# Attention and MLP on one core: weights of 64-key blocks laid as [hi | lo], two products in place of three, and a new plan

## The chip, the cores and the metric

The kernel runs on one core of a Trainium2 chip. The metric is the time on the device of one execution in microseconds, the median of three runs. Five engines run side by side: TensorE (PE; its weight loads are shown apart, as PEld), VectorE (DVE), ScalarE (ACT), GpSimd (POOL), and SyncE (SP), which issues all transfers here.

## What is computed

Eight batches, eight heads, 576 positions of 64 features: attention with a mask by blocks of 64 (a query sees its own block of keys and those before it), then for all 4608 tokens a layer of 512 to 2048 with h * tanh(softplus(h)), and one back to 512. All in float32.

```python
scores = scale * np.matmul(q, k.transpose(0, 1, 3, 2))
mask = block_i >= block_j                  # block = position // 64
scores = np.where(mask, scores, -1000000000.0)
attn = np.exp(scores - np.max(scores, axis=-1, keepdims=True))
attn = attn / (np.sum(attn, axis=-1, keepdims=True) + 1e-09)
x = np.matmul(attn, v)                     # heads side by side: 4608 x 512
h = x @ w_in
g = h * np.tanh(np.log1p(np.exp(h)))
out = g @ w_out
```

## The kernel before

Products of two float32 matrices are made of float16 parts: each operand is split into hi and lo, and hi*hi, hi*lo and lo*hi are summed on TensorE. Batch 0 is an exception; its attention runs in float32 while the weights are loaded and split. For batches 1 to 7, heads are taken in pairs, four pairs a batch, 28 pairs in all. For a pair:

- `load_pair` loads q, k (`ql`, `kl`) and v (`VL`, L850) and splits them: hi by ScalarE or VectorE (L909, L913: `QH`, `KH`, `VH`), lo by VectorE (L917: `QL`, `KL`, `VO`). `VL` has 7 blocks of 128 rows of v: 0 to 2 are full, 3 holds two separate blocks of 64 keys, and 4, 5, 6 hold one block of 64 keys with zeros in the other half. `VH` has a column of ones for the sums of the weights, zero where the keys are.
- `attend_pair` runs the 576 queries in three rounds r = 0, 1, 2. Scores go to PSUM (L1202, L1214), VectorE takes the maxima (L1243, L1251), ScalarE the exponentials into a float32 tile `pe` (L1277). The weights are split into hi and lo by one operation each of 1024 columns for two heads: hi on ScalarE, VectorE or GpSimd (L1309, L1314), lo on VectorE (L1326). Both stand in a tile `P` (`P2`), and a DMA transposes it into `PT` (L1333), keys on the partitions. The last 64 queries of round 1 are transposed once more, as "r = 3", into `PL` (L1348).
- `values` (L1381) multiplies the transposed weights with v: `SEEN` lists, for each half, the blocks (round, block of weights, block of v) that each group of 128 queries sees. Each of them takes three products per head: hi with `VH`, hi with `VO`, lo with `VH`. A block of weights has 128 columns of keys; where only 64 of the keys belong to it, v has zeros in the other half (blocks 4, 5, 6).
- `weigh` divides by the sums and splits the result into `xt`, which a DMA transposes into `x`.

The MLP of 576 tokens is two tiles of 384 and 192 tokens: `m1` (L1559), the activation on ScalarE (L1588), the split into `Gt` (L1620, L1629, L1635), `m2` (L1664), and the store.

No order is written out by hand. Every step is an `Op` with an engine (some with a choice of engines), an estimated duration, and what it comes after. `Plan` gives each a due time out of the table `DUE`, runs a list schedule by these, and emits all engines' queues in the order that comes out. So the numbers in `DUE` alone set which step stands before which in each queue. Tiles are handed around in rings: two `pe`, two `P2`, four `PT`, one `PL`, two score tiles `ss`, one `u`.

Of the kernel before, what the change touches and what calls it, by code (L numbers as in the profile page):

```python
# [30 lines left out]
    "w": ((-61.5, -2, 296, 15.5), (96.5, 301, 329, 293.5)),  # L31
    "batch": (134.5, 54, 455.5, 305.5, 387.5, 808, 492, 726.5),
    "load": (
        (83.5, -32, 600.5, 570),
        (36, 483.5, 361.5, -83.5),
        (276, 346.5, 611, 481.5),
        (565, 598, 494.5, 672.5),
        (648.5, 658, 422.5, 604),
        (343, 499, 528.5, 422.5),
        (661.5, 543, 581, 672),  # L40
        (519.5, 843, 510.5, 637.5),
        (757.5, 795, 760, 591.5),
    ),
    "tile": (
        (-51, -125.5, -73.5, -80.5, -51, -47.5, -51, -26.5,
         319, 223.5, 300.5, 333, 81.5, -56.5, 375,
         314.5, 398.5, 467, 26.5, 342, 505.5, 522),
        (19.5, 249.5, 135.5, 297.5, 196.5, -21.5, 316, 400.5,
         604.5, 539.5, 679, 458.5, 343, 123.5, 283.5,
         267, 250.5, 470, 358, -216, 356.5, -75),  # L50
        (320, 282.5, 449, 284, 681, 964, 780, 427,
         447, 435.5, 624, 399.5, 375.5, 484, 386.5,
         320.5, 409.5, 543, 531.5, 375, 412.5, 340),
        (483, 31, 275.5, 339.5, 292.5, 104, 293, 625,
         84.5, 303.5, 373.5, 407, 379.5, -72.5, 127,
         404, 404.5, 421, 565.5, -125.5, 356, -251.5),
        (448.5, 373.5, 590, 365.5, 434.5, 336.5, 446.5, 284,
         357.5, 489.5, 428, 310, 292.5, -42, 410,
         513.5, 777.5, 590, 613, 604, 709.5, 639.5),
        (372.5, 551, 292.5, 381.5, 476.5, 835, 556, 396.5,  # L60
         724, 871, 821, 711.5, 554.5, 463.5, 309,
         893, 680.5, 615, 529, 515, 441.5, 30),
        (373, 388, 435, 502.5, 260, 301.5, 656.5, 579,
         297.5, 503, 548, 528, 666, 511, 332,
         627, 392, 426, 519.5, 752, 584.5, 605.5),
        (368, 598.5, 373, 367.5, 583, 554.5, 411, 406,
         237.5, 328.5, 607.5, 573, 674.5, -33.5, 787,
         729, 772.5, 818.5, 923.5, 63.5, 469.5, -66),
        (389, 453, 304.5, 478, 715, 634, 371.5, 693.5,
         348, 796.5, 774, 602.5, 855.5, 503, 530,  # L70
         776, 701.5, 819, 590, 813, 895, 812.5),
        (634.5, 956, 494.5, 795, 1165, 830.5, 1058, 709,
         710, 839.5, 692.5, 741.5, 725, 247.5, 944.5,
         560, 629.5, 1001, 527.5, -160, 671, -106),
        (802.5, 973, 1047, 434.5, 658.5, 854, 632, 826,
         762, 798, 686, 941, 746.5, 271.5, 1046.5,
         667, 865, 1006, 611, 643, 1168.5, 645),
        (832, 643.5, 951.5, 1059, 547.5, 819, 763.5, 866,
         699, 730.5, 1083.5, 1171.5, 1010.5, -12, 856,
         594.5, 1149, 860.5, 1071.5, -34, 790, -55.5),  # L80
        (944.5, 712, 595.5, 736, 871.5, 785.5, 960.5, 607,
         692, 788, 586.5, 1165.5, 977.5, 12.5, 753,
         572.5, 900.5, 937.5, 839.5, 768.5, 725.5, 796.5),
        (1028.5, 640, 726, 558, 695.5, 664, 1160.5, 1140.5,
         1094.5, 925, 768.5, 853, 1007, -98, 1008,
         1061.5, 723, 870, 774.5, -89, 1203.5, 261.5),
        (950.5, 896.5, 636, 989.5, 884, 689.5, 926, 1069,
         955.5, 1107, 1099.5, 940.5, 677.5, -156, 1045.5,
         851.5, 705.5, 754.5, 1035.5, 839, 1052, 1161),
        (794, 1058.5, 678.5, 694.5, 811.5, 1135, 639, 810.5,  # L90
         937.5, 1100.5, 1138.5, 870.5, 1130.5, -151.5, 1101,
         876, 1045, 1214.5, 1347.5, 355.5, 1319.5, 461),
# [255 lines left out]
def attention_moe(  # L348
# [87 lines left out]
    PL = [const.tile([P, 4, P], F16, name=f"PL{i}") for i in range(NPL)]  # L436
# [382 lines left out]
    def load_pair(b, p, i, wait_s, wait_u):  # L819
# [80 lines left out]
        v_part = VL.rearrange("p c (a d) -> p c a d", d=D), m["VH"][:, :, :, 0:D], m["VO"]  # L900
        for j, (parts, s, ns, after) in enumerate((
            (q_parts, sc[:, 0:1], (S - 64, P), [sco]),
            ([(kl, m["KH"], m["KL"])], sc[:, 1:2], (S,), [sco]),
            ([v_part], s_x, (KV * P,), [batches[b]["sx"]] + v_ins + wait_u),
# [10 lines left out]
            def lows(parts=parts, s=s):  # L915
                for src, hi_, lo_ in parts:
                    nc.vector.scalar_tensor_tensor(  # L917
                        out=lo_, in0=src, scalar=s, in1=hi_, op0=ALU.mult, op1=ALU.subtract
                    )
# [8 lines left out]
            lo = add("dve", sum(dve(n) + 0.06 for n in ns), lows, [hi])  # L928
# [31 lines left out]
    def attend(p, half, st):  # L960
# [133 lines left out]
        for a in range(2):  # L1094
# [81 lines left out]

    SEEN = (
        (
# [3 lines left out]
        ),  # L1182
        (((0, 0, 0), (0, 1, 5)), ((1, 0, 5),)),
    )

    def attend_pair(b, p, st):
# [83 lines left out]
        for r in range(3):  # L1270
# [33 lines left out]
            def both(r=r):  # L1304
                t = P2[his[r].slot].rearrange("p (k z a q) -> p z a k q", z=2, a=2, q=P)
                return t[:, 0], t[:, 1], pe[ex[r].slot].rearrange("p (a k q) -> p a k q", a=2, q=P)

            def part(op, both=both):
                return lambda: op(out=both()[0], in_=both()[2])  # L1309

            hi = add(
                "act",
                act(1024) + 0.09,
                lambda both=both: nc.scalar.copy(both()[0], both()[2]),  # L1314
# [3 lines left out]
                    ("dve", dve(1024, fast=True), part(nc.vector.tensor_copy)),  # L1318
                    ("pool", 1.05, part(nc.gpsimd.tensor_copy)),
# [5 lines left out]
                dve(1024) + 0.08,  # L1325
                lambda both=both: nc.vector.tensor_sub(both()[1], both()[2], both()[0]),  # L1326
# [17 lines left out]
            if r == 1:  # L1344
                late = add(
                    "sp",
                    TURN_LATE,
                    lambda: nc.sync.dma_start(  # L1348
                        out=PL[late.slot][:, :, 64:P],
                        in_=P2[his[1].slot][64:P, 0 : 4 * P],  # L1350
                        transpose=True,
                    ),
                    [lo, tr],
                    take=[pl_ring],
                    free=[(p2_ring, hi)],
                )
                tr.free, tr.frees = [], []
                last["T"] = late
# [3 lines left out]
        for half in (1, 0):  # L1362
# [3 lines left out]
            def values(half=half, seen=seen):  # L1366
# [3 lines left out]
                for j, bs in enumerate(seen):  # L1370
                    for a in range(2):
                        for r, k, vb in bs:
                            if r == 3:
                                h, l = (PL[late.slot][:, 2 * z + a] for z in range(2))
# [3 lines left out]
                            o = uv[:, j, a]  # L1378
                            vh, vo = m["VH"][:, vb, a], m["VO"][:, vb, a]
                            for out, p_, v_ in ((o, h, vh), (o[:, 0:D], h, vo), (o, l, vh)):  # L1380
# [12 lines left out]
                products([E] * (6 * sum(len(x) for x in seen))),  # L1393
# [339 lines left out]
    TURN, TURN_LATE, TURN_X = (2.7, 0.5), (1.3, 0.3), ((3.8, 0.9), (1.4, 0.5))  # L1733
# [100 lines left out]
```

## Time and profile before

| | us |
|---|---|
| median of three runs | 1007.91 (1007.24 to 1011.48) |
| the profiled execution | 1007.62 |
| its span, first to last instruction | 1005.5 |
| TensorE busy | 986.4 |
| ScalarE busy | 664.4 |
| VectorE busy | 662.2 |
| GpSimd busy | 83.5 |

The span is what the trace shows; 2.1 us lie around it. Busy times are of the whole span, over stages with different limits: until about 140 us the weights are prepared and batch 0 runs, then pairs and MLP tiles run mixed, and after about 850 us only MLP is left. Matmuls overlap, so the duration of one is not what one costs.

### The profile page before, as it was taken

The numbers are of one execution on the slowest core, as the hardware profiler recorded it, in microseconds if no ns is written. First come the engines' busy times: TensorE is split into PE (matmuls) and PEld (weight loads), VectorE is DVE, ScalarE is ACT, GpSimd is POOL, SyncE is SP. The second block draws the span as 40 slices with busy tenths as digits, with TensorE's granted clock in tenths as the row PEclk, the third lists the DMA queues.
The fourth block names the chain that finished last, engine by engine and source line by source line (L and its number), as shares of the span: only waits on it lengthen the run. The fifth ranks groups of instructions, "written<-read, shape, count | busy, mean of one in ns | idle before, by whom it ended". The sixth has DMA issues, their size and how long they took to land.

```text
span 1005.5 us, 25329 instructions
## 1 busy us (share of the span) xinstructions
PE 986.4 (98%) x10856; PEld 734.6 (73%) x10856; DVE 662.2 (66%) x1288; ACT 664.4 (66%) x1042; POOL 83.5 (8%) x111
## 2 busy tenths in 40 slices
PE   8999899999999999999999999999999999999998
PEld 6677467786678688686778766877678866877787
DVE  5999998989878527875469677885568784220210
ACT  2769887768869747777579676885858676332221
POOL 1000311102000001100001010110011210000000
PEclk9999899999999999999999999999999999999999
DMA  9763657796568326693486936693358843320000
GB/s 324 245 191 109 167 101 164 150 198 120 119 147 157 77 36 162 137 195 62 86 147 135 181 77 137 139 179 52 72 120 165 142 93 65 61 56 1 25 17 25
DMA packets 276850, 121.59 MB, mean 121 GB/s; under 512 B 224513, under 2 KB 262913, under 8 KB 276737
## 3 DMA queue, kind: packets, MB, share of 16 engines
q1 hardware_dynamic: 276736, 119.96, 54.5%
q8 instruction: 85, 1.39, 0.6%
q14 instruction: 29, 0.23, 0.1%
HBM read 55.18 MB, written 9.44 MB: 64 GB/s over the span
## 4 chain that ended last, share of the span: by engine, by line
PE 87%; DVE 8%; ACT 2%; issue 2%; DMA 1%; SPq 1%; DVEq 0%; ACTq 0%
PE acc L1664 36%; PE acc L1559 33%; PE u L1381 7%; PE ss L1202 5%; PE u L1139 2%; DVE Gt L603 1%; PE ss L1067 1%; DVE pv L1243 1%; DVE P L1326 1%; PE acc L996 1%; DMA PT<-P 1%; PE acc L667 1%; DVE wo_l L694 1%; PE ss L996 1%; PE ss L1106 0%
## 5 line engine op out<-in xcount | busy, mean ns | idle before, releaser
L1559 PE MATMUL acc<-x,wi_h 128*128 128x192 f16 (+1 forms) x2048 | 393.5, 287 | 0.7 <-DVE ot L1696 0.3
L1664 PE MATMUL acc<-Gt,wo_h 128*128 128x192 f16 (+1 forms) x2048 | 383.7, 286 | 2.2 <-DVE ot L1696 1.2
L1559 PE MATMUL acc<-x,wi_l 128*128 128x192 f16 (+1 forms) x1024 | 293.8, 287 | 0.0
L1664 PE MATMUL acc<-Gt,wo_l 128*128 128x192 f16 (+1 forms) x1024 | 292.9, 286 | 0.0
L1559 PEld LDWEIGHTS <-wi_h 128*128 128x128 f16 x2048 | 191.1, 98 | 81.3 <-issue 5.8
L1664 PEld LDWEIGHTS <-wo_h 128*128 128x128 f16 x2048 | 187.5, 98 | 54.3 <-issue 4.3
L1588 ACT ACTIVATE Et<-acc,bv 128x384 f32<-128x384 f32 x192 | 109.0, 578 | 106.1 <-PE acc L1559 105.2
L1277 ACT ACTIVATE pe<-ss,pv 128x192 f32<-128x192 f32 (+1 forms) x280 | 148.7, 605 | 18.5 <-DVE pv L1251 10.5
L1635 DVE SCALAR_TENSOR_TENSOR Gt<-Et,bv,Gt 128x1536 f16<-128x1536 f32 (+1 forms) x64 | 90.8, 1425 | 105.4 <-ACT Gt L1620 105.2
L1664 PEld LDWEIGHTS <-wo_l 128*128 128x128 f16 x1024 | 100.2, 98 | 34.3 <-issue 1.3
L1559 PEld LDWEIGHTS <-wi_l 128*128 128x128 f16 x1024 | 100.5, 98 | 33.6 <-issue 0.8
L1243 DVE TENSOR_REDUCE pv<-ss 128x2 f32<-128x384 f32 (+4 forms) x140 | 106.0, 790 | 19.1 <-PE ss L1214 18.7
L1326 DVE TENSOR_TENSOR P<-pe,P 128x1024 f16<-128x1024 f32 x84 | 102.9, 1225 | 12.7 <-ACT P L1314 7.6
L1381 PEld LDWEIGHTS <-PT 128*128 128x128 f16 x2352 | 79.7, 98 | 4.7 <-issue 0.6
L1381 PE MATMUL u<-VH,PT 128*128 128x65 f16 x1568 | 82.8, 194 | 0.0
L1381 PE MATMUL u<-VO,PT 128*128 128x64 f16 x784 | 79.4, 193 | 0.0
L1277 ACT ACT_TABLE_LOAD x57 | 73.1, 1283 | 8.4 <-DVE pv L1251 5.5
L1588 ACT ACT_TABLE_LOAD x59 | 75.7, 1283 | 1.0
L1620 ACT ACTIVATE Gt<-Et,bv 128x768 f16<-128x768 f32 (+1 forms) x53 | 64.8, 1224 | 15.7 <-PE acc L1664 14.6
L1703 ACT ACTIVATE ot<-acc,bv 128x384 f32<-128x384 f32 (+1 forms) x37 | 17.6, 501 | 60.9 <-PE acc L1664 47.1
L1202 PEld LDWEIGHTS <-QH 64*128 64x128 f16 x896 | 27.5, 95 | 26.6 <-issue 14.0
L1309 DVE CAST P<-pe 128x1024 f16<-128x1024 f32 x32 | 22.8, 714 | 34.0 <-DMA PT<-P 23.6
(129 smaller groups left out, 1007.5 us busy)
## 6 DMA issues: line engine op xcount, KB each, us to landing
out_dram<-ot SPq DMA_DIRECT2D x48, 192.0 KB, 2.4
wo_l<-in_w_in_dram SPq DMA_DIRECT2D x8, 1024.0 KB, 6.3
Gt<-in_w_out_dram SPq DMA_DIRECT2D x16, 512.0 KB, 4.2
kl<-in_v_dram SPq DMA_DIRECT2D x28, 288.0 KB, 3.1
ql<-in_q_dram SPq DMA_DIRECT2D x28, 288.0 KB, 3.4
kl<-in_k_dram SPq DMA_DIRECT2D x28, 288.0 KB, 3.3
VL<-in_v_dram SPq DMA_DIRECT2D x28, 192.0 KB, 2.7
VL<-in_v_dram SPq DMA_DIRECT2D x28, 96.0 KB, 2.9
```

Source lines behind the costliest of these rows:

```text
L996: nc.tensor.matmul(bank(a)[:, col : col + n], lhsT=m["QF"][hs, q : q + P], rhs=m["KF"][hs, key : key + n], start=first, stop=True, skip_gr ...
L1202: nc.tensor.matmul(ss[:, 512 * a + col : 512 * a + col + n], lhsT=m[q_][hs, at : at + P], rhs=m[k_][hs, key : key + n], start=first, stop= ...
L1243: nc.vector.reduce_max(out=mx[:, c], in_=ss[:, :, c0:c1], axis=mybir.AxisListType.X)
L1277: nc.scalar.activation(pe[ex[r].slot][:, cols], ss_[S0[r].slot % NSS][:, cols], AF.Exp, scale=esc, bias=mx[:, c, a : a + 1],)
L1309: return lambda: op(out=both()[0], in_=both()[2])
L1326: lambda both=both: nc.vector.tensor_sub(both()[1], both()[2], both()[0]),
L1381: nc.tensor.matmul(out, lhsT=p_, rhs=v_, start=first, stop=True, skip_group_check=True,)
L1559: nc.tensor.matmul(pt, lhsT=w[:, d, f * P : (f + 1) * P], rhs=x[:, d, :], start=k == 0 and d == 0 and z == 0, stop=d == NP - 1 and z == 2, ...
L1588: nc.scalar.activation(Et[:, (self.i * NG + g) % NE, j : j + K, 0:n], acc_[c.slot % NACC][:, 0 : K * n].rearrange("p (k n) -> p k n", k=K) ...
L1620: lambda g_hi=g_hi, ev=ev: nc.scalar.activation(g_hi, ev, AF.Copy, scale=self.s_g),
L1635: lambda g_hi=g_hi, g_lo=g_lo, ev=ev: nc.vector.scalar_tensor_tensor(out=g_lo, in0=ev, scalar=self.s_g, in1=g_hi, op0=ALU.mult, op1=ALU.su ...
L1664: nc.tensor.matmul(pt, lhsT=w[:, f, o * P : (o + 1) * P], rhs=g, start=k == 0 and f == 0 and z == 0, stop=f == NF - 1 and z == 2, skip_gro ...
```

## The change

Only batches 1 to 7 are touched. Where a block of weights has 64 keys, its 128 columns become hi and lo of the same 64 keys, side by side, so that after the transpose hi is on partitions 0 to 63 and lo on 64 to 127. The block of v it meets has the same 64 rows twice: `VH` is [hi | hi], `VO` is [lo | 0]. Two products are left: the pair with `VH` gives hi*hi + lo*hi, with `VO` hi*lo. This is done for block 1 of round 0 and block 0 of round 1 (`MIXED`), and hence for "r = 3"; five of the 15 entries of `SEEN` get a fourth number, which half of the keys.

The split of the weights is then done in pieces, as the mixed block has another layout: three for round 0, two for round 1, one for round 2. v has 6 blocks; it takes four loads instead of three, and its lo two operations (four blocks on 128 partitions, two on 64). `PL` holds two blocks instead of four. The table `DUE` is new throughout, and the estimated durations of the changed steps are adapted.

```diff
 DUE = {
-    "w": ((-61.5, -2, 296, 15.5), (96.5, 301, 329, 293.5)),
+    "w": ((-53.5, -7.5, 92, 14.5), (645, 263, 668.5, 387)),
...
-    KV = 7
+    KV = 6
     VL = const.tile([P, KV, P], F32, name="VL")
-    nc.gpsimd.memset(VL[64:P, 4:6, :], 0.0)
-    nc.gpsimd.memset(VL[0:64, 6, :], 0.0)
...
-        nc.gpsimd.memset(m["VH"][64:P, 4:6, :, D:E], 0.0)
-        nc.gpsimd.memset(m["VH"][0:64, 6, :, D:E], 0.0)
+        nc.gpsimd.memset(m["VO"][64:P, 4:6], 0.0)
...
-    PL = [const.tile([P, 4, P], F16, name=f"PL{i}") for i in range(NPL)]
+    PL = [const.tile([P, 2, P], F16, name=f"PL{i}") for i in range(NPL)]
...
-            (VL[64:P, 3:7:3], vb[S - 64 :].unsqueeze(1).to_broadcast([64, 2, P]), 64),
+            (VL[64:P, 3:6:2], vb[S - 64 :].unsqueeze(1).to_broadcast([64, 2, P]), 64),
+            (VL[64:P, 4], vb[S - P : S - 64], 64),
...
-            ([v_part], s_x, (KV * P,), [batches[b]["sx"]] + v_ins + wait_u),
+            (
+                [(vl, vh, None)],
+                list(zip(*v_parts)),
+                s_x,
+                (KV * P,),
+                (4 * P, 2 * P),
+                [batches[b]["sx"]] + v_ins + wait_u,
+            ),
...
+    MIXED = (1, 0, None)
...
-            ((0, 1, 6), (0, 2, 0), (0, 3, 1)),
-            ((1, 0, 6), (1, 1, 0), (1, 2, 1), (1, 3, 2)),
-            ((2, 0, 3), (2, 1, 0), (2, 2, 1), (2, 3, 2), (3, 0, 4)),
+            ((0, 1, 5, 1), (0, 2, 0), (0, 3, 1)),
+            ((1, 0, 5, 1), (1, 1, 0), (1, 2, 1), (1, 3, 2)),
+            ((2, 0, 3), (2, 1, 0), (2, 2, 1), (2, 3, 2), (3, 0, 4, 0)),
         ),
-        (((0, 0, 0), (0, 1, 5)), ((1, 0, 5),)),
+        (((0, 0, 0), (0, 1, 5, 0)), ((1, 0, 5, 0),)),
...
+            mix = MIXED[r]
+            runs = ((0, 1), (2, 4)) if mix else ((0 if mix is None else 1, 4),)
+
+            def pieces(r=r, mix=mix, runs=runs):
+                flat, src = P2[his[r].slot], pe[ex[r].slot]
+                t = flat.rearrange("p (k z a q) -> p z a k q", z=2, a=2, q=P)
+                x = src.rearrange("p (a k q) -> p a k q", a=2, q=P)
+                for k0, k1 in runs:
+                    yield t[:, 0, :, k0:k1], t[:, 1, :, k0:k1], x[:, :, k0:k1]
+                if mix is not None:
+                    t = flat.rearrange("p (k h a z q) -> p k z a h q", h=2, a=2, z=2, q=64)
+                    x = src.rearrange("p (a k h q) -> p k a h q", a=2, h=2, q=64)
+                    yield t[:, mix, 0], t[:, mix, 1], x[:, mix]
+
+            def each(op, pieces=pieces):
+                def emit():
+                    for h, _, x in pieces():
+                        op(out=h, in_=x)
+
+                return emit
+
+            def rest(pieces=pieces):
+                for h, l, x in pieces():
+                    nc.vector.tensor_sub(l, x, h)
...
-                        in_=P2[his[1].slot][64:P, 0 : 4 * P],
+                        in_=P2[his[1].slot][64:P, 0 : 2 * P],
...
-                            for out, p_, v_ in ((o, h, vh), (o[:, 0:D], h, vo), (o, l, vh)):
+                                hl = h if which == [0] else l
+                            prods = [(o, hl, vh), (o[:, 0:D], hl, vo)]
+                            if not which:
+                                prods = [(o, h, vh), (o[:, 0:D], h, vo), (o, l, vh)]
+                            for out, p_, v_ in prods:
```

## Rows read from the trace of the kernel before

**Rows 1.** The page: busy us (share of the span) and instructions by engine
```profile
PE 986.4 (98%) x10856; PEld 734.6 (73%) x10856; DVE 662.2 (66%) x1288; ACT 664.4 (66%) x1042; POOL 83.5 (8%) x111
```
**Rows 2.** The page: the chain that ended last, by engine
```profile
PE 87%; DVE 8%; ACT 2%; issue 2%; DMA 1%; SPq 1%; DVEq 0%; ACTq 0%
```
**Rows 3.** Busy time by stretches of 25 us; the first row names the columns
```profile
core 0: us, PE busy (x) PEld busy (x) DVE busy (x) ACT busy (x) POOL busy (x), PEclk, DMA share, GB/s
...
100.00:125.00 25.00, 20.40 (x148) 11.37 (x146) 24.73 (x48) 20.27 (x32) 8.27 (x6) 0.86 0.67 167
125.00:150.00 25.00, 22.67 (x278) 16.29 (x277) 24.69 (x35) 22.62 (x34) 4.31 (x4) 1.00 0.53 95
...
175.00:200.00 25.00, 23.83 (x317) 18.47 (x315) 23.15 (x53) 19.06 (x34) 2.72 (x5) 1.00 0.72 145
...
850.00:875.00 25.00, 25.00 (x289) 19.42 (x288) 4.65 (x11) 6.46 (x12) 0.00 (x0) 1.00 0.35 62
```
**Rows 4.** TensorE's waits: waiter <- waited for: us, times, longest
```profile
PE acc L996 <- DMA Et<-in_k_dram: 4.6, 1, 4.6
PE ss L1202 <- DVE KL L917: 2.6, 1, 2.6
PE ss L1202 <- DVE QH L913: 2.0, 1, 2.0
```
**Rows 5.** Busy time by stretches of 4 us, columns as in rows 3
```profile
116.00:120.00 4.00, 2.47 (x21) 1.52 (x21) 4.00 (x7) 3.34 (x6) 0.00 (x0) 0.56 0.49 155
120.00:124.00 4.00, 4.00 (x16) 1.92 (x15) 3.96 (x8) 1.97 (x6) 1.24 (x1) 0.58 0.56 108
```
**Rows 6.** The chain in order of time, 70 to 150: start, us, what
```profile
93.01 0.73 DVE KL L917
...
106.34 1.13 DVE P L1326
...
128.45 0.92 DVE QL L917 x2
...
142.81 5.85 PE acc L1664 x35
```
**Rows 7.** The line of the products: duration ns min/median/max, first and last start
```profile
L1381 PEld LDWEIGHTS <-PT x2352: 95/98/103, 130.2 to 880.0; 128*128 128x128 f16 x196
...
L1381 PEld LDWEIGHTS <-PL x168: 96/98/101, 140.8 to 880.1; 128*128 128x128 f16 x168
```
**Rows 8.** The chain in order of time, whole span: the products of one pair
```profile
163.79 2.17 PE u L1381 x72
```
**Rows 9.** Groups of instructions, shapes apart: count, busy us, mean ns, idle before
```profile
L917 DVE SCALAR_TENSOR_TENSOR QL<-ql,pv,QH 128x128 f16<-128x128 f32 x28 | 10.7, 382 | 0.0
```
**Rows 10.** The casts of the weights by engine: duration ns min/median/max, first and last start
```profile
L1309 DVE CAST P<-pe x32: 679/694/997, 164.9 to 845.4; 128x1024 f16<-128x1024 f32 x32
L1309 POOL CAST P<-pe x25: 1037/1078/2576, 101.0 to 822.3; 128x1024 f16<-128x1024 f32 x25
...
L1314 ACT CAST P<-pe x27: 1028/1045/1080, 114.2 to 846.7; 128x1024 f16<-128x1024 f32 x27
```
**Rows 11.** Groups of instructions in the first 150 us
```profile
L1309 POOL CAST P<-pe 128x1024 f16<-128x1024 f32 x4 | 7.9, 1983 | 28.9 <-ACT pe L1277 24.1 <-issue 4.9
...
L1326 DVE TENSOR_TENSOR P<-pe,P 128x1024 f16<-128x1024 f32 x6 | 7.3, 1217 | 0.0
```
**Rows 12.** SP's issues of transposes and of v's loads: duration ns min/median/max
```profile
L1333 SPq DMA_TRANSPOSE PT<-P x84: 1317/2730/3908, 107.5 to 865.1; - x84
...
L1348 SPq DMA_TRANSPOSE PL<-P x28: 1170/1211/2447, 122.7 to 862.6; - x28
...
L850 SPq DMA_DIRECT2D VL<-in_v_dram x84: 368/606/1418, 19.0 to 806.9; - x84
```
**Rows 13.** Groups of instructions, shapes apart, whole span: GpSimd's casts
```profile
L1309 POOL CAST P<-pe 128x1024 f16<-128x1024 f32 x25 | 34.7, 1388 | 123.1 <-ACT pe L1277 48.8 <-issue 20.0 <-DMA PT<-P 18.5
...
L1466 POOL CAST xt<-tt 128x384 f16<-128x384 f32 x13 | 13.3, 1024 | 127.7 <-DVE tt L1445 125.8 <-DVE bv L767 1.8
...
L1466 POOL CAST xt<-tt 128x256 f16<-128x256 f32 x13 | 9.6, 737 | 105.1 <-DVE tt L1445 104.5 <-DVE wv L500 0.6
```

More of the change, by code (lines that the diff above doesn't have):

```diff
@@ new lines @@
+        (41, 305.5, 102.5, 400.5, 28, -32, 375.5, 539,
+         592, 443, 744, 381.5, 377, 391, 277.5,
+         175, 197.5, 411.5, 274, -302.5, 321, -98),
+        (315.5, 290, 495.5, 375, 370.5, 1057, 778, 351,
+         512.5, 519.5, 798, 524, 773, 476.5, 512,
+         317, 435, 676, 658, 433.5, 401.5, 330),
+        (556, 28.5, 43.5, 267.5, 271, 246.5, 357, 631,
+         78.5, 354.5, 335.5, 437.5, 368.5, -81, 131.5,
+         346.5, 484, 458, 450.5, -175.5, 259, -164),
+        (499, 409, 666, 287.5, 361.5, 346, 584.5, 335.5,
+         410.5, 580.5, 432, 328.5, 456, -17, 480.5,
+         803, 688, 639.5, 703, 535, 795.5, 716),
@@ new lines @@
+        (375.5, 527, 655.5, 634.5, 283.5, 770, 564.5, 346,
+         425, 319, 858, 637.5, 494.5, 350.5, 351.5,
+         929, 577, 311.5, 608.5, 548, 597.5, 159),
+        (306.5, 431, 500, 483.5, 571.5, 1003.5, 781.5, 774,
+         365, 672, 681.5, 628.5, 660.5, 502.5, 476,
+         685, 408, 626.5, 522.5, 753.5, 818.5, 612),
+        (433.5, 846, 424.5, 516.5, 719, 718, 500.5, 370.5,
+         291, 514, 709.5, 645.5, 739.5, 11.5, 1009.5,
+         871.5, 834, 978.5, 960.5, -56, 497.5, 184),
@@ new lines @@
+        (439.5, 516, 278.5, 523, 696, 408, 425.5, 656,
+         339.5, 783, 867, 642.5, 943, 496, 707.5,
+         635.5, 556.5, 683, 526.5, 854.5, 1014, 576),
+        (593.5, 821.5, 469.5, 708, 1061.5, 887, 1110.5, 767.5,
+         934, 825.5, 611.5, 831.5, 550.5, 183, 942,
+         665, 465, 1008.5, 532, -321, 616, -132.5),
+        (795.5, 1021, 1212.5, 461, 796.5, 965, 738, 804.5,
+         543.5, 1015, 850.5, 1107.5, 800, 351, 1100,
+         641.5, 827, 830, 518.5, 520, 1157, 626),
+        (840, 631.5, 963.5, 1028, 1010, 859, 729.5, 885.5,
+         715.5, 640, 1192, 1173, 978.5, -42, 1032.5,
+         604.5, 1306, 972.5, 1169.5, 147.5, 750.5, -88.5),
@@ L899, in load_pair @@
         ]
[L900 to L903, printed above, removed]
-            ([v_part], s_x, (KV * P,), [batches[b]["sx"]] + v_ins + wait_u),
+        k_parts = [(kl, m["KH"], m["KL"])]
+        vl, vh = VL.rearrange("p c (a d) -> p c a d", d=D), m["VH"][:, :, :, 0:D]
+        v_parts = [(x[:, 0:4], x[low, 4:6]) for x in (vl, vh, m["VO"])]
+        for j, (parts, lo_parts, s, ns, lo_ns, after) in enumerate((
+            (q_parts, q_parts, sc[:, 0:1], (S - 64, P), (S - 64, P), [sco]),
+            (k_parts, k_parts, sc[:, 1:2], (S,), (S,), [sco]),
+            (
[6 more added lines that the diff above has]
+            ),
         )):
@@ L913, in hi_dve, with lows @@
                     nc.vector.tensor_scalar_mul(hi_, src, s)
-            def lows(parts=parts, s=s):
+            def lows(parts=lo_parts, s=s):
                 for src, hi_, lo_ in parts:
                     nc.vector.scalar_tensor_tensor(
-                        out=lo_, in0=src, scalar=s, in1=hi_, op0=ALU.mult, op1=ALU.subtract
+                        out=lo_,
+                        in0=src,
+                        scalar=s[0 : src.shape[0]],
+                        in1=hi_,
+                        op0=ALU.mult,
+                        op1=ALU.subtract,
                     )
@@ L927, in load_pair @@
             )
-            lo = add("dve", sum(dve(n) + 0.06 for n in ns), lows, [hi])
+            lo = add("dve", sum(dve(n) + 0.06 for n in lo_ns), lows, [hi])
             last[j] = lo
@@ L1301, in attend_pair @@
             his = st.setdefault("hi", [])
[L1304 to L1309, printed above, removed]
+            mix = MIXED[r]
[18 more added lines that the diff above has]
+                    nc.vector.tensor_sub(l, x, h)
+            ns = [256 * (k1 - k0) for k0, k1 in runs] + [256] * (mix is not None)
             hi = add(
                 "act",
-                act(1024) + 0.09,
-                lambda both=both: nc.scalar.copy(both()[0], both()[2]),
+                sum(act(n) for n in ns) + 0.09,
+                each(nc.scalar.copy),
                 [ex[r]] + scaled_all,
@@ L1317, in attend_pair @@
                 other=[
-                    ("dve", dve(1024, fast=True), part(nc.vector.tensor_copy)),
-                    ("pool", 1.05, part(nc.gpsimd.tensor_copy)),
+                    ("dve", sum(dve(n, fast=True) for n in ns), each(nc.vector.tensor_copy)),
+                    ("pool", 0.96 + 0.09 * len(ns), each(nc.gpsimd.tensor_copy)),
                 ],
@@ L1324, in attend_pair @@
                 "dve",
-                dve(1024) + 0.08,
-                lambda both=both: nc.vector.tensor_sub(both()[1], both()[2], both()[0]),
+                sum(dve(n) for n in ns) + 0.04,
+                rest,
                 [hi],
@@ L1371, in values @@
                     for a in range(2):
-                        for r, k, vb in bs:
+                        for r, k, vb, *which in bs:
+                            o = uv[:, j, a]
+                            vh, vo = m["VH"][:, vb, a], m["VO"][:, vb, a]
                             if r == 3:
-                                h, l = (PL[late.slot][:, 2 * z + a] for z in range(2))
+                                hl = PL[late.slot][:, a]
                             else:
@@ L1392, in attend_pair @@
                 "pe",
-                products([E] * (6 * sum(len(x) for x in seen))),
+                products([E] * sum(4 if len(y) > 3 else 6 for x in seen for y in x)),
                 values,
```

87 lines of the change are left out of this document (26 added, 61 removed).

## The prediction, made before the change was run

> **What bounds the kernel now.** I read four views, from coarse to fine. First the page's busy times: TensorE works 986.4 of 1005.5 us, VectorE and ScalarE about two thirds [rows 1]. Then the chain that ended last: 87% of it is TensorE and 8% VectorE [rows 2]. So a microsecond taken from TensorE is nearly a microsecond of the span, except where the chain leaves it. The third view, busy time by stretches of 25 us, says where that is [rows 3]: TensorE lacks 4.60 us in 100:125, 2.33 in 125:150 and 1.17 in 175:200, and VectorE is 99% busy in the first two. From 850 on VectorE is nearly free and TensorE is full. The fourth, TensorE's waits, names the two largest there: scores of a pair that wait for KL and QH, which VectorE makes [rows 4]. [...] In the chain, VectorE carries the path up to 142.81, where the second product of the first tile starts; from there it is TensorE with small breaks [rows 6]. The kernel is thus bound by TensorE, behind a start bound by VectorE whose holes cost 4.60 + 2.33 + 1.17 + 2.8 = 10.9 us. That sum is used twice below.
>
> **The products: what is removed.** Per pair, values() runs 15 blocks for two heads with three products each: 90, and 28 pairs make 2520, which is the count of weight loads [rows 7]. Five of the 15 blocks (the two with r = 0 and r = 1 against block 6, the late one, and two of half 1) hold 64 keys and now take two products: 2 x 5 = 10 fewer per pair, 280 in all. The 194 ns that the page shows for one product is its latency; they overlap. The price is the spacing: the chain holds 72 of them in 2.17 us [rows 8], 30.1 ns each. 280 x 30.1 = **8.4 us**. They lie on the engine that sets the end, and nothing takes their place there, as the two products left are the same shapes as before.
>
> [...]
>
> **The splits of the weights: what is added.** Until now one cast and one subtraction of 1024 columns made hi and lo of a round. Now round 0 has three of each (256 + 512 + 256), round 1 two (768 + 256), round 2 one: 3 more casts and 3 more subtractions per pair, the columns unchanged. What a piece costs apart from its columns isn't in the trace for this line, so I take the nearest rows [rows 6]: a 1024 subtraction advances the chain by 1.13 us, 1.1 ns per column; KL, one piece of 576, by 0.73; QL, two pieces of 512 + 128, by 0.92. The extra 64 columns are 0.07, so the second piece is 0.12. The lower bound is 0 (more work in more pieces can't be less), the upper about 0.25, what a 128-column piece costs beyond its columns as a duration of its own (0.382 less 0.14) [rows 9]. I take 0.12, because it is the advance, not the duration. VectorE: 3 x 0.12 = 0.36 per pair, and for the casts, of which it does 32 of 84 [rows 10], 3 x 32/84 x 0.12 = 0.14. V's split shrinks from 896 to 768 columns (-0.14 at 1.1 ns) but its lo has two pieces (+0.12): nothing. Together 0.5 per pair, 14 us over 28 pairs, 2 to 3% of VectorE's time. From 200 on its idle time covers this. Without cover, in the start, it is on the path: by 150 us six subtractions have run [rows 11], of which four (both rounds with pieces of the first pair, its round 2, and round 0 of the second) stand in the chain before 142.81, and carry 2 + 1 + 0 + 2 = 5 more pieces: 5 x 0.12 = **+0.6** (bounds 0 and 1.3). A second, weaker place is 175:200, with three or so more pieces: **+0.3**. And what TensorE saves before 142.81 is not collected, since VectorE sets that point: one pair, 10 x 30 ns = **+0.3**.
>
> [...]
>
> ScalarE casts 27 of 84 and GpSimd 25 [rows 10]. ScalarE's third of idle time hides 27 pieces; GpSimd has over 900 us idle, but who waits for its result isn't free: see the third rival.
>
> **Loads and transposes.** VL gets a fourth load per pair: 0.61 us more of SP's time, 28 times, ahead of whatever transpose comes next on that queue; the late transpose goes from four blocks to two, and its 1.21 us [rows 12] fall by perhaps 0.25 (2.73 for 16 blocks against 1.21 for 4: 0.13 a block). Net +0.35 us per pair on a queue that mostly waits for its inputs; no TensorE wait in [rows 4] names it, so I cost it at 0. If that cover goes, in a chain that ends at a transpose, it is 0.35 each time. The memsets of the start move from VL to VO on GpSimd, while TensorE waits for its first loads: 0.
>
> **The new plan.** All due times are different, so the order of every queue is too. It takes nothing away by itself; it redraws the 10.9 us of holes. Bounds: none left (-10.9), or twice (+10.9). Nothing in the trace says which, and I take 0.
>
> **Sum.** -8.4 + 0.6 + 0.3 + 0.3 = -7.2. Against the profiled execution of 1007.62 us that is 1000.4; the median is 0.29 above that execution, so I say 1000.5.
>
> **The rivals.**
> 1. *The new order also closes holes of the start.* For it: 10.9 us lie there, and the wait for KL stands behind weight preparation that nobody needs yet. Against: VectorE is 99% busy from 100 to 150, so work must be moved out of it, not only reordered, and the change adds some. Half of the holes: -7.2 - 5.5 gives 995. Chance 0.17.
> 2. *The start gets longer.* [...] Half of the holes once more, less what was already counted: +4.5 on the sum gives 1005. [...] Chance 0.22.
> 3. *GpSimd's pieces turn it slower than before.* GpSimd's casts of 256 and 384 columns take 0.74 and 1.02 us in the mean, one of 1024 1.39 [rows 13]: they hardly get cheaper with size. Three pieces at 0.74, 1.1 and 0.74 are 2.6 us, 1.2 more than the one cast; the subtraction waits for it, it holds one of two pe buffers, the exponentials wait for those and hold the scores. In the start four casts ran there, at 1.98 each [rows 11]. The gain is eaten when 6 to 7 of the 25 lie on the path (8.4 / 1.2); with 12 it is 1007.6 - 8.4 + 14.4 = 1013.6. Against: TensorE has other tiles to work on after 200. Chance 0.06.
> 4. *The removed products were hidden.* They would be if the chain ran elsewhere; with 87% on TensorE this holds only in the start, and is counted. No chance of its own.
>
> **How the numbers follow.** Forecast 0.55, its own range 997.5 to 1003; rival 1 0.17, rival 2 0.22, rival 3 0.06. The range 994 to 1006 leaves out the part of rival 1 that closes over half of the holes (0.08), rival 3, and a little of rival 2 (0.03). About half a percent, 5 us, is what a measurement of this kernel can tell from no change. Faster by more means under 1002.9: most of the forecast (0.53) and rival 1, 0.70. Within it: rival 2 and the rest, 0.24. Slower: 0.06.
>
> **What the profile would show.** Right: 2240 weight loads on the products' line, 66 products in some 2.0 us; TensorE busy about 978; TensorE full from 200 on; 168 subtractions instead of 84, VectorE some 14 us busier at most; holes between 100 and 200 as before. Wrong: TensorE's busy time falls by 8 and the span doesn't, then the holes grew (rival 2: look at the granted clock between 100 and 150) or TensorE waits for scores behind a GpSimd cast (rival 3). If the span falls by more than 9, holes closed. If the busy time doesn't fall by 8, the spacing of products changed.

## The result

The changed kernel takes 998.92 us (998.13 to 999.86) against 1007.58 (1006.94 to 1011.48) for the kernel before on the same chip: a ratio of 0.9906, 95% interval 0.988 to 0.9933, or 8.7 us less. The forecast was 1000.5, range 994 to 1006, faster. Its profiled execution is one of 998.63 us with a span of 996.9 us.

The page of the changed kernel, beside [rows 1] and [rows 2]: busy us by engine, then the chain that ended last.

```profile
PE 973.1 (98%) x10576; PEld 722.2 (72%) x10576; DVE 668.5 (67%) x1411; ACT 663.4 (67%) x1062; POOL 115.0 (12%) x166
...
PE 86%; DVE 9%; DMA 2%; issue 1%; ACT 1%; SPq 1%; ACTq 0%; DVEq 0%
```

TensorE has 280 products fewer (10856 to 10576) and 13.3 us less to do; VectorE has 6.3 us more and GpSimd 31.5.

What moved where is seen best if the span is cut at the first product of the second layer. It starts at 141.42 us before and at 141.45 after (the 142.81 of the prediction is where the chain passes from VectorE to TensorE, some products later). That VectorE sets this point is shown by e6 below. Busy time in the two stretches, kernel before first, then the changed one (columns as in [rows 3]):

```profile
0.00:141.40 141.40, 128.72 (x1140) 93.52 (x1141) 126.22 (x270) 101.34 (x154) 17.92 (x35) 0.98 0.68 199
141.40:1005.40 864.00, 857.68 (x9723) 641.11 (x9718) 535.98 (x1019) 563.04 (x889) 65.61 (x76) 1.00 0.53 108
```
```profile
0.00:141.40 141.40, 121.82 (x1130) 89.03 (x1130) 126.69 (x277) 105.89 (x160) 25.09 (x39) 0.98 0.70 196
141.40:996.80 855.40, 851.27 (x9451) 633.16 (x9446) 541.81 (x1135) 557.52 (x903) 89.94 (x127) 1.00 0.54 110
```

In the start, TensorE has 6.9 us less to do and the start is as long as it was. As starts differ by several us between executions, the agreement to 0.03 us is chance; that they are about equal is all that can be read from it. All 8.6 us of these two executions come from the second stretch: TensorE's work falls by 6.4 us, and its idle time there (with the tail, the last evacuation and store) from 6.3 to 4.1.

TensorE's waits, beside [rows 4], and stretches of 4 us around the cut, beside [rows 5]:

```profile
PE acc L1008 <- DMA Et<-in_k_dram: 4.7, 1, 4.7
PE ss L1217 <- DVE KH L920: 4.7, 1, 4.7
```
```profile
136.00:140.00 4.00, 0.61 (x6) 0.29 (x7) 3.88 (x12) 3.15 (x3) 1.34 (x1) 0.51 0.42 95
140.00:144.00 4.00, 3.40 (x23) 1.79 (x23) 3.97 (x8) 4.00 (x6) 0.00 (x0) 0.50 0.49 147
144.00:148.00 4.00, 4.00 (x31) 3.08 (x30) 4.00 (x5) 1.55 (x4) 3.38 (x2) 0.71 0.89 141
```

The large hole is of the same kind as before, scores that wait for KH from VectorE, and the granted clock falls behind it again, to 0.51 and 0.50; but the hole has moved from 112 to 133, to just ahead of the cut, so that the first products of the second layer run at a granted clock of 0.50 until 146 (0.86 in 146:147, 1.00 from 147 on).

### The profile page after: what moved, and what is told of

It reads as the page before. It is cut to its first block, busy times and chain, and to the rows that moved or that the text cites. A ratio compares the mean times of both kernels' runs of the same rounds, so it can differ in the third digit from the quotient of the medians.

```text
span 996.9 us, 25050 instructions
## 1 busy us (share of the span) xinstructions
PE 973.1 (98%) x10576; PEld 722.2 (72%) x10576; DVE 668.5 (67%) x1411; ACT 663.4 (67%) x1062; POOL 115.0 (12%) x166
## 4 chain that ended last, share of the span: by engine, by line
PE 86%; DVE 9%; DMA 2%; issue 1%; ACT 1%; SPq 1%; ACTq 0%; DVEq 0%
PE acc L1702 37%; PE acc L1597 35%; PE u L1419 7%; PE ss L1217 6%; DVE Gt L600 1%; DVE wo_h L600 1%; DMA x<-xt 1%; DVE wo_l L691 1%; DMA wo_l<-in_w_in_dram 1%; DVE PT L1045 1%; PE u L1151 1%; DVE pv L1258 1%; DMA PT<-P 1%; DVE P L1342 0%; DVE wi_l L691 0%
## 5 line engine op out<-in xcount | busy, mean ns | idle before, releaser
L1342 DVE TENSOR_TENSOR P<-pe,P 128x256 f16<-128x256 f32 (+1 forms) x168 | 110.8, 700 | 14.9 <-ACT P L1336 13.3
L1336 POOL CAST P<-pe 128x256 f16<-128x256 f32 (+3 forms) x81 | 60.3, 777 | 201.9 <-DMA PT<-P 79.2
L1419 PEld LDWEIGHTS <-PT 128*128 128x128 f16 x2128 | 72.8, 98 | 5.1 <-issue 0.6
L1419 PE MATMUL u<-VH,PT 128*128 128x65 f16 x1344 | 74.3, 193 | 0.0
L1419 PE MATMUL u<-VO,PT 128*128 128x64 f16 x784 | 72.6, 193 | 0.0
L1741 ACT ACTIVATE ot<-acc,bv 128x192 f32<-128x192 f32 (+1 forms) x46 | 21.1, 487 | 66.8 <-PE acc L1702 52.9
L1217 PEld LDWEIGHTS <-QH 64*128 64x128 f16 x896 | 27.4, 95 | 28.7 <-issue 13.5
```

The costliest lines, as they stand in the source:

```text
L1217: nc.tensor.matmul(ss[:, 512 * a + col : 512 * a + col + n], lhsT=m[q_][hs, at : at + P], rhs=m[k_][hs, key : key + n], start=first, stop= ...
L1336: op(out=h, in_=x)
L1342: nc.vector.tensor_sub(l, x, h)
L1419: nc.tensor.matmul(out, lhsT=p_, rhs=v_, start=first, stop=True, skip_group_check=True,)
L1741: evac(lambda o, i, s: nc.scalar.activation(o, i, AF.Copy, scale=s))
```

## The experiments

An execution's start varies by several us, as is shown at the end, so two numbers are given for each kernel: the ratio of the timed runs to the kernel before, and, from the trace, the cut and the rest of the span behind it. Most kernels keep the queues' order as it was in the kernel they are made from (a step is changed, its estimate in the plan isn't); the exceptions are the two that swap the table. A ratio is taken over all timed runs of a kernel and those of the kernel before that ran beside it, so it isn't the quotient of two medians of this table.

| | median, us | ratio to before (95%) | cut at | rest of span | TensorE busy in it |
|---|---|---|---|---|---|
| before | 1007.58 | | 141.4 | 864.0 | 857.7 |
| changed | 998.92 | 0.9906 (0.988 to 0.9933) | 141.4 | 855.4 | 851.3 |
| e1, products only | 1001.79 | 0.9925 (0.9897 to 0.9954) | 138.9 | 857.9 | 849.9 |
| e2, pieces only | 1008.02 | 1.0005 (0.998 to 1.0031) | 145.3 | 863.8 | 857.6 |
| e9, both, old order | 998.16 | 0.9918 (0.9884 to 0.9952) | 138.5 | 857.1 | 849.8 |
| e5, changed, third product back | 1005.80 | 0.9990 (0.9967 to 1.0014) | 139.4 | 864.4 | 859.4 |
| e3, changed, old table | 1008.59 | 0.9998 (0.9976 to 1.002) | 139.1 | 868.9 | 858.0 |
| e4, before, new table | 1010.38 | 1.0042 (1.0018 to 1.0065) | 142.0 | 866.1 | 861.2 |
| e6, start's subtractions twice | 1003.80 | 0.9970 (0.9946 to 0.9995) | 149.9 | 856.8 | 851.7 |
| e7, late subtractions twice | 1029.52 | 1.0234 (1.0188 to 1.028) | 145.0 | 886.8 | 858.2 |
| e10, late pieces twice | 1000.50 | 0.9933 (0.9909 to 0.9957) | 143.7 | 857.2 | 851.4 |
| e8, GpSimd's casts twice | 1005.67 | 0.9988 (0.9962 to 1.0015) | 142.1 | 861.2 | 852.8 |
| e11, work put in the hole | 997.46 | 0.9904 (0.9873 to 0.9935) | 141.9 | 855.5 | 850.6 |

### The products alone, the pieces alone, and both

e1 is the kernel before with two products on the five entries:

```diff
-    for out, p_, v_ in ((o, h, vh), (o[:, 0:D], h, vo), (o, l, vh)):
+    prods = ((o, h, vh), (o[:, 0:D], h, vo), (o, l, vh))
+    for out, p_, v_ in prods[: 2 if vb > 3 else 3]:
```

> The kernel before, order of all queues unchanged, with the third product (lo with VH) left out on the five 64-key blocks of each pair; that part of the sum is missing from the output. Theory, that the span pays for each product by its spacing on TensorE: 27 of the 28 pairs lie behind the start that VectorE sets, so 27 x 10 x 30.1 ns = 8.1 us less, a ratio of 0.992; the first second-layer product still starts at 141.4 us; holes on TensorE stay at 11 us or grow by under 1. Rival, that most of the gain of the change came from the new plan: under 4 us less, ratio above 0.996, as holes open where the products were.

e2 cuts the splits of the weights:

```diff
-    def part(op, both=both):
-        return lambda: op(out=both()[0], in_=both()[2])
+    def part(op, both=both, cuts=((0, 1, 2, 4), (0, 1, 4), (0, 4))[r]):
+        def emit():
+            h, l, x = both()
+            for k0, k1 in zip(cuts, cuts[1:]):
+                op(h[:, :, k0:k1], l[:, :, k0:k1], x[:, :, k0:k1])
+        return emit
...
```

The casts and the subtraction are then all made by `part`.

> The kernel before, order unchanged, with the casts and subtractions of the weights cut into pieces: round 0 at 256 + 256 + 512 columns, round 1 at 256 + 768, as many as in the changed kernel; products, layout and v unchanged. Theory: a further subtraction costs 0.065 us (three of them advanced by 1.26 us in the chain of the changed kernel against 1.13 for one of 1024), so the start gets 5 x 0.065 = 0.3 us longer, the first second-layer product starts at 141.7 instead of 141.4 us, and the total rises by under 1 us, ratio 0.999 to 1.002. Rival, pieces of GpSimd on the path: 5 us or more, ratio above 1.005, with TensorE's waits behind GpSimd's casts.

e9 has both edits.

> The kernel before with its order unchanged, the third product left out on the 64-key blocks (that part of the sum is missing) and the splits of the weights in pieces: both parts of the change without a new plan and without the new layout. Theory, that the parts add up and an order that fits is all that is needed: 8.1 - 0.3 us less than before, ratio 0.990 to 0.996, like with the products alone. Rival, that the pieces need the new plan: ratio above 0.998.

Measured: 0.9925, 1.0005 and 0.9918. The products alone bring the gain, the pieces cost nothing that the timed runs can tell, and together they give as much as the whole change, all within intervals of about 3 us either way. In the rest of the span TensorE's work falls by 7.8 us in e1 and 7.9 in e9, where 270 x 30.1 ns = 8.1 was expected; the span keeps 6.1 and 6.9 of that, and 1.7 and 1.0 come back as idle time. The changed kernel keeps 8.6 there, 1.7 more than e9; that may be the new order's, but one trace of each and the timed runs don't settle it. The cut of e2, at 145.3 and not 141.7, isn't the pieces' doing: the difference enters at 58 us, before the first piece runs, in a stretch from 48 to 58 that had the clock at 0.5 in this execution.

What a piece costs is read from the chain of the changed kernel: three subtractions of 256 + 512 + 256 columns, then three of 768 + 256 and 1024.

```profile
107.30 1.26 DVE P L1342 x3
```
```profile
118.09 2.33 DVE P L1342 x3
```

One of 1024 took 1.13 [rows 6]. So two more pieces cost 0.13 and one more 0.07 (2.33 less 2 x 1.13): 0.065 us each. Over the whole run the busy time of the subtractions grows by more, from 102.9 us to 110.8 for 84 more pieces, 0.09 each.

### The third product put back

```diff
-    prods = [(o, hl, vh), (o[:, 0:D], hl, vo)]
+    prods = [(o, hl, vh), (o[:, 0:D], hl, vo), (o[:, 0:D], hl, vo)]
```

> The changed kernel, order unchanged, with a third product of the same shape back on the five 64-key entries (the one with VO runs twice, so that this part is counted twice in the output). Theory: 280 x 30.1 ns = 8.4 us more than the changed kernel, 1007 us, ratio to before 0.997 to 1.002; TensorE has no holes behind the start to take them. Rival, that the new plan left room: under 4 us more, ratio below 0.995.

Measured: 1005.80, ratio 0.9990, against 0.9906 for the changed kernel: 8.5 us by the difference of the two ratios. In the trace the larger of the two groups of a pair's products goes back from 66 in 1.99 us to 72 in 2.17; first the changed kernel, then e5:

```profile
164.37 1.99 PE u L1419 x66
```
```profile
162.26 2.17 PE u L1419 x72
```

TensorE's work behind the cut rises from 851.27 to 859.40 us, 8.13, which is 270 x 30.1 ns to the digit; the rest of the span rises by 9.0. Taken out or put back, in two different orders, the products cost their spacing.

### The two tables swapped

e3 is the changed code with the old `DUE`, e4 the old code with the new one; the plan is made anew from the table in both.

> The changed kernel with the table of due times of the kernel before, so that the plan is made anew from the old times. Theory, that the gain is the products and the table only moves holes about: 998 to 1002 us, ratio 0.990 to 0.995. Rival, that the new table is needed for the gain: 1003 us or more, with more than 15 us of holes on TensorE.

> The kernel before with the table of due times of the changed kernel. Theory: 1006 to 1011 us, ratio 0.998 to 1.003, since the same work runs on TensorE. Rival, that the new table brings the gain: 1003 us or less, ratio below 0.996.

e3 came out at 1008.59, e4 at 1010.38. The theory's 998 to 1002 for e3 is missed, and so is the rival's reading: the rival held that the new table brings the gain, and e4 shows that on the old code it brings none, but costs 4. What falls is the thought that an order needs no fitting. In e3 TensorE waits more:

```profile
PE acc L1597 <- ACT Et L1626: 5.9, 7, 2.1
PE acc L1702 <- ACT Et L1626: 5.9, 1, 5.9
```

The two rows are not in the changed kernel in that size: one hole of 5.9 us just ahead of the cut, and 5.9 in seven others, 3.0 of them behind it (the first row was 2.7 there, all ahead of the cut; the second isn't in its list). The rest of the span is 13.5 us longer than with the new table: TensorE is idle 6.8 us longer, and busy 6.7 longer, as 107 more of its instructions stand behind the cut, 66 of them products of the first pair and 24 of the first layer. This second part is largely work moved out of the start, so the 13.5 overstate the loss, and the timed runs give it. The gain thus needs an order that fits the new operations: the old order kept as it was (e9), or the new table. The wrong table costs about 9 us (0.9998 against 0.9906), as much as the products bring.

### VectorE: in the start, and behind it

e6 does the subtractions twice in the first two pairs, e7 in the 24 pairs of batches 2 to 7, e10 only one piece of 256 columns in rounds 0 and 1 of those.

```diff
     def rest(pieces=pieces):
-        for h, l, x in pieces():
-            nc.vector.tensor_sub(l, x, h)
+        for _ in range(2 if b == 1 and p < 2 else 1):
+            for h, l, x in pieces():
+                nc.vector.tensor_sub(l, x, h)
```

That is e6; in e7 the condition is `b > 1`. e10 has the old loop and, behind it:

```diff
+        if b > 1 and mix is not None:
+            nc.vector.tensor_sub(l, x, h)
```

> The changed kernel, order unchanged, with the subtractions of the weights' lo done twice in the first two pairs (same result). Theory, that VectorE sets the start: the four rounds that stand before the first second-layer product (1.26 + 1.20 + 1.13 + 1.26) put it off by 4.8 us, and the total rises by 4 to 5, to about 1003.5, ratio 0.994 to 0.998. Rival, that the start has slack on VectorE: under 1.5 us more, ratio below 0.993.

> The changed kernel, order unchanged, with the subtractions of the weights' lo done twice in the 24 pairs of batches 2 to 7 (same result): 24 x 3.7 = 90 us more work on VectorE. Theory, that VectorE's idle time covers its work behind the start: under 3 us more than the changed kernel, ratio to before 0.990 to 0.994. Rival, that VectorE, busy for 22 to 24 of 25 us between 225 and 325, is a second bound there: 8 us or more, ratio above 0.999, with holes on TensorE between 225 and 350.

> The changed kernel, order unchanged, with one subtraction of 256 columns done twice in rounds 0 and 1 of the pairs of batches 2 to 7 (same result): 48 x 0.33 = 16 us more on VectorE, about what the prediction had put down for all pieces. Theory, that idle time covers a dose of that size though not 90 us: under 2 us more than the changed kernel, ratio to before 0.990 to 0.994. Rival, that the cost is in proportion to the 30 us of the run with 90 us more: 5 us, ratio 0.995 to 0.998.

e6: 1003.80, 4.9 more than the changed kernel by the medians and 6.4 by the ratios, where 4 to 5 was expected. Its trace has a partner: e7 has the same order and the same work up to the cut, and the same low clock between 20 and 36 (0.53 and 0.52). The cut is at 149.9 in e6 and 145.0 in e7: 4.9 us for 4.9 of VectorE's work (131.8 us busy up to the cut against 126.9). The start is VectorE's, and pays in full.

e7: 1029.52, 31 us more by the medians, where under 3 was expected; the theory fell and the rival holds. Behind the cut VectorE is 86.5 us busier than in the changed kernel and the span 31.4 longer; 24.5 of these are idle time of TensorE. TensorE's largest wait, a wait of ScalarE, and two stretches of 50 us:

```profile
PE ss L1217 <- ACT pe L1292: 14.8, 12, 2.4
```
```profile
ACT L1292 <- DVE P L1343: 29.0, 15, 4.5
```
```profile
250.00:300.00 50.00, 45.48 (x538) 30.96 (x536) 47.44 (x101) 34.22 (x63) 8.65 (x12) 1.00 0.63 133
300.00:350.00 50.00, 44.96 (x605) 36.76 (x603) 48.73 (x102) 36.53 (x58) 10.35 (x13) 1.00 0.73 149
```

VectorE is 95 and 97% busy there: the subtraction frees a `pe` buffer late, the exponentials wait for it (29.0 us, against 2.7 in the changed kernel), and the scores wait for the exponentials to free `ss`. VectorE's 314 us of idle time behind the cut in the changed kernel are of no use here: 121 of them lie after 850, and between 200 and 300 there are 13.

e10: 19.1 us more of VectorE behind the cut, 1.8 more of span, 0.9933 against 0.9906. The theory (under 2) fits the trace, the ratio lies in its range and its interval reaches into the rival's. A dose of this size costs a tenth of itself, one of 86.5 more than a third.

### GpSimd's casts twice

```diff
-    ("pool", 0.96 + 0.09 * len(ns), each(nc.gpsimd.tensor_copy)),
+    ("pool", 0.96 + 0.09 * len(ns), each(nc.gpsimd.tensor_copy, 2)),
```

The 2 makes `each` run its pieces twice.

> The changed kernel, order unchanged, with every cast of the weights that GpSimd does done twice (same result): 81 pieces more, about 60 us more of GpSimd. Theory, that GpSimd's pieces cost nothing behind the start and little in it: at most 3 us more than the changed kernel, ratio to before 0.990 to 0.995. Rival, that its casts stand on the path (the third rival of the prediction): 8 us or more, ratio above 0.999.

1005.67, ratio 0.9988: about 8 us by the ratios, 5.8 in the rest of the span. That is nearly the rival's number and far over the theory's. But casts on the path aren't all that the trace shows. The stretch behind the cut in e8, to be read beside the changed kernel's row of the result (141.40:996.80):

```profile
142.10:1003.30 861.20, 852.79 (x9451) 633.73 (x9446) 556.75 (x1135) 557.48 (x903) 142.89 (x200) 1.00 0.52 109
```

GpSimd is 53 us busier than there, and VectorE 14.9 us, with the same 1135 instructions: in this execution they take longer. It isn't all of them. Two of VectorE's groups behind the cut, QL's lo, which reads SBUF alone, and the maxima, which read the scores from PSUM; changed kernel, then e8:

```profile
L924 DVE SCALAR_TENSOR_TENSOR QL<-ql,pv,QH 128x512 f16<-128x512 f32 x25 | 19.3, 771 | 0.7 <-ACT QH L916 0.7
L1258 DVE TENSOR_REDUCE pv<-ss 128x2 f32<-128x1024 f32 x26 | 31.6, 1216 | 0.0
```
```profile
L924 DVE SCALAR_TENSOR_TENSOR QL<-ql,pv,QH 128x512 f16<-128x512 f32 x25 | 21.4, 855 | 0.7 <-ACT QH L916 0.7
L1258 DVE TENSOR_REDUCE pv<-ss 128x2 f32<-128x1024 f32 x26 | 31.6, 1214 | 0.0
```

The first takes 855 ns in the mean and not 771, the second what it took. What makes the one longer and not the other isn't shown. How much of the 5.8 comes from the longer instructions, and how much from the subtraction's wait for its cast, isn't told apart here.

### Work put in the hole

20 matmuls of no use stand before the scores that wait for KH:

```diff
+    for _ in range(20 if (b, p, r) == (1, 2, 0) else 0):
+        nc.tensor.matmul(ss[:, 0:448], lhsT=wi_h[:, 0, 0:P], rhs=wi_h[:, 0, 0:448], ...)
```

> The changed kernel, order unchanged, with 20 matmuls of 448 columns of no use put on TensorE before the scores of the third pair, where it waits 4.7 us for KH and its granted clock then falls to 0.5 until 147. They write score columns that are overwritten. [...] Rival, that VectorE sets the pace there whatever the clock: within 1 us of the changed kernel, 0.990 to 0.993.

Stretches of 4 us of e11, to be read beside those of the changed kernel in the result:

```profile
136.00:140.00 4.00, 2.30 (x17) 1.05 (x15) 3.83 (x15) 3.12 (x4) 1.34 (x2) 1.00 0.45 99
140.00:144.00 4.00, 2.19 (x21) 1.16 (x21) 4.00 (x6) 4.00 (x4) 0.32 (x1) 0.71 0.50 147
144.00:148.00 4.00, 4.00 (x35) 3.06 (x34) 3.97 (x6) 2.44 (x7) 3.05 (x2) 0.87 0.77 108
```

997.46, ratio 0.9904: no difference from the changed kernel that these runs could tell, though an interval of 3 us either way doesn't exclude the theory, that the low clock costs time on the path and 2 to 3 us fall off with the clock at 1.0. The trace doesn't show them. The edit did only part of what it was for: the clock is full up to 140 (0.51 there in the changed kernel), but it is still low for a few us around the cut (0.71 in 140:144, 0.87 in 144:148); TensorE is busy 2.30 and 2.19 of 4 us there. Behind the cut, at 141.9, TensorE has 0.7 us less to do and waits 0.8 longer: the rest of the span is 855.5 as it was. VectorE is busy 3.83, 4.00 and 3.97 of 4 there, which fits the rival, that it sets the pace. Whether the low clock would cost anything with VectorE out of the way stays open.

## Why the prediction was right, point by point

The sum said -7.2 us; the spans of the two profiled executions differ by -8.6. The mechanism, products paid by their spacing on the engine that sets the end, held. The small terms were partly wrong, and some of the agreement is luck, as the points say: of the 1.4 us between the two numbers, the +0.6 for pieces in the start can't be seen, and the stretch behind it fell by 8.6 where 8.1 less 0.3 was forecast.

**The bound and the products: right, for the reason given.** 66 products take 1.99 us and 72 take 2.17, the spacing of 30.1 ns that the sum used. The line has 2240 weight loads (2128 and 112). TensorE's work behind the cut moves by -7.8 (e1), -7.9 (e9) and +8.1 (e5) with the products alone. In the changed kernel two tiles make up nearly all of the -6.4 there: `u`, which the products write, and `acc`, which the MLP's matmuls write. TensorE's busy time on `u` behind the cut, before and changed, and then on `acc` (columns: stretch, busy us and count, granted clock, DMA share, GB/s):

```profile
141.40:1005.50 864.10, 82.50 (x2437) 1.00 0.53 108
```
```profile
141.40:996.90 855.50, 74.14 (x2160) 1.00 0.54 110
```
```profile
141.40:1005.50 864.10, 733.96 (x5904) 1.00 0.53 108
```
```profile
141.40:996.90 855.50, 736.15 (x5904) 1.00 0.54 110
```

The products give 8.4, for 277 of them: the 270 of 27 pairs are 8.1, and the last seven of the first pair stood behind the cut before. `acc`, with the same 5904 matmuls, takes 2.2 back; its first ones run at the low clock, and 3.38 busy us at 0.50 and 5.00 at 0.87 up to 150 us lose 2.3, an estimate from these rows:

```profile
141.40:145.00 3.60, 3.38 (x15) 0.50 0.46 149
145.00:150.00 5.00, 5.00 (x41) 0.87 0.98 164
```

Idle time gives 2.2, and 0.2 are left over. Hence 8.6. Pieces, holes and clock together thus cost nothing behind the cut, where the sum had put 0.3; that the lower clock and the closed holes are of one size is luck.

**The first pair, +0.3: right.** What TensorE saves ahead of the cut isn't collected: its busy time fell by 6.9 us in the start and the start is no shorter, and e6 shows that VectorE sets it. One pair's ten products are 0.3 of the 6.9. 2.5 are 24 products of batch 0's attention, which the change doesn't touch and which took 1.9 times as long in the execution of before. TensorE's groups between 13 and 22 us, before and then changed:

```profile
L1139 PE MATMUL u<-Et,pe 128*128 128x65 f32 x24 | 5.4, 420 | 0.0
```
```profile
L1151 PE MATMUL u<-Et,pe 128*128 128x65 f32 x24 | 2.9, 277 | 0.0
```

The granted clock reads 1.00 in both there, so what made them slower isn't shown; where the rest of the 6.9 comes from I have not taken apart. The forecast "TensorE busy about 978" (973.1 came) missed by work in the start that bought no time. The us that count are those behind the cut.

**The pieces: right in kind, twice too large.** The step took 0.12 us for a piece, from QL against KL; the pieces themselves show 0.065 in the chain. The 0.6 us in the start is 0.33, too little to be seen in where the cut lies, and VectorE's work grows by 6.3 us and not 14. Part of that difference is that the new plan sends 81 of the 168 pieces to GpSimd; before, it had 25 of 84 casts [rows 10]. The second place, +0.3 in 175:200, wasn't there: TensorE is busy 25.00 of 25 us in that stretch, and the hole of 1.17 us that [rows 3] had there is closed.

```profile
175.00:200.00 25.00, 25.00 (x256) 18.30 (x254) 17.81 (x48) 18.09 (x32) 1.55 (x2) 1.00 0.77 152
```

**"From 200 on its idle time covers this": true here, too loose as a rule.** e10 adds 19.1 us of VectorE's work behind the cut and pays 1.8, e7 adds 86.5 and pays 31.4. VectorE is 87% busy between 200 and 300, and its share of the whole span, 67%, doesn't tell that. The step held because 5.8 us over 27 pairs is a small dose.

**The new plan at 0, bounds 10.9 either way: the value right, by luck.** The step said that no row decides and took the middle. e9, with the old order, gives the same gain within the intervals. But e3 shows that an order that fits badly costs about 9 us, near the bound, and with the new order come two effects of 2.2 us that happen to cancel. That the new table fits the new operations is what the 0 needed, and the prediction had no row for it.

The 10.9 us were also no price. 2.8 of them are no hole but the author's estimate of work lost at the granted clocks of 0.56 and 0.58 [rows 5], 2.47 x 0.44 + 4.00 x 0.42; no run shows that term, and e11, with the clock at 1.00 in 136:140 where the changed kernel has 0.51, reaches the cut no earlier, at 141.9 us against 141.4. Of the 8.1 us of holes in the 10.9, all but 2.2 lay ahead of the cut, where VectorE sets the time. After the change TensorE lacks 9.4 us between 100 and 150, where it lacked 6.9 before [rows 3], the clock is low there again (0.80 in 125:150), and the kernel is faster all the same:

```profile
100.00:125.00 25.00, 22.30 (x204) 13.04 (x203) 24.72 (x46) 23.64 (x37) 7.39 (x8) 1.00 0.78 180
125.00:150.00 25.00, 18.27 (x210) 13.73 (x207) 24.52 (x47) 21.11 (x30) 9.08 (x7) 0.80 0.55 97
```

**The rivals.** The first, holes that close, is half true: behind the cut they go from 6.3 to 4.1 us with the tail, but the large one ahead of the cut stayed, and the low clock behind it now falls on the MLP: -2.2 and +2.2. The second didn't come: the start isn't longer, though a hole of 4.7 us at 133 and a granted clock of 0.51 and 0.50 behind it are both in the trace. The third had its premise right in kind, that these casts hardly get cheaper with size. GpSimd's casts after the change, all of the line and all sizes in one row (duration ns min/median/max):

```profile
L1336 POOL CAST P<-pe x81: 396/616/2551, 103.0 to 820.2; 128x256 f16<-128x256 f32 x44, 128x512 f16<-128x512 f32 x15, 128x768 f16<-128x768 f32 x14, 128x1024 f16<-128x1024 f32 x8
```

The sizes take 0.62, 0.64, 1.02 and 1.47 us in the mean, so that three pieces are 1.9 us and not 2.6. Its price was too high: 53 us more of these casts cost 5.8 to 8 us, a tenth to a seventh, where the rival let up to half of the casts, 12 of 25, count in full.

**Loads and transposes at 0.** No wait of TensorE names `VL`, `PT` or `PL` after the change either. One in the start names a transpose of `x`, on the same queue:

```profile
PE acc L1597 <- DMA x<-xt: 1.4, 1, 1.4
```

That transpose landed 9.8 us after its issue at 56, and 8.0 us after it in e5, which has the same order and no such wait. So it is a difference between executions, and not shown to be the change's.

## What to carry to other kernels

Price overlapping matmuls by their spacing in the chain of waits, and count only those in stretches where the chain is TensorE's: that gave 8.1 us for 27 pairs, and put back they cost 8.1 of TensorE's work. A hole in a stretch that another engine sets is no price. An engine's idle share over the span, here a third, is no cover where it is 87% busy locally; ask how large the dose is in the stretch that pays. An order made for one set of operations doesn't carry over: with the wrong table, a gain of 9 us was gone, so after such a change either keep the order as it was or make it anew, and time both.

## What the runs showed of the hardware

Two things weren't expected. The granted clock of the start differs between executions in which nothing differs up to there. Changed kernel, e5, e7 and e10 have the same order and work up to the cut, but for e5's third products; it lies at 141.4, 139.4, 145.0 and 143.7 us. The stretch 20:36 of the changed kernel, then of e7:

```profile
20.00:36.00 16.00, 13.71 (x137) 11.14 (x134) 15.12 (x34) 10.08 (x16) 0.64 (x1) 1.00 0.95 308
```
```profile
20.00:36.00 16.00, 16.00 (x96) 12.85 (x94) 10.93 (x27) 7.51 (x11) 0.40 (x1) 0.52 0.83 270
```

At 0.52 TensorE did 96 instructions in 16.00 busy us, at 1.00 137 in 13.71, and VectorE, which waits for its results, fell behind with it. It was 0.68 in e10 and 1.00 in e5. e2 and the kernel before, alike up to the first split of weights at 101 us, differ in the same way, here in 52:56, before and then e2:

```profile
52.00:56.00 4.00, 4.00 (x33) 2.41 (x32) 3.83 (x9) 2.17 (x4) 0.00 (x0) 1.00 0.84 277
```
```profile
52.00:56.00 4.00, 4.00 (x11) 2.54 (x12) 3.44 (x8) 0.60 (x2) 0.00 (x0) 0.50 0.83 280
```

The cuts of the changed kernel, e5, e7 and e10 lie up to 5.6 us apart. Not all of that is the clock: the changed kernel and e5 both have it at 1.00 up to 132 us and lie 2.0 apart, and 1.5 of these arise right behind the wait for the transpose of `x` at 65, which only the changed kernel has. The timed runs of the kernel before scatter over 1003.2 to 1014.9; that the clock explains all of that isn't shown. This scatter is why the rest of the span behind the cut tells these kernels apart better than one execution's time.

The second is that VectorE's instructions took longer with more work on GpSimd: behind the cut of e8 14.9 us more for 53 us more of GpSimd's, with the same 1135 instructions. QL's lo took 855 ns in place of 771, the maxima over 1024 columns, which read the scores from PSUM, 1214 and before 1216.
